# Mirrored rows in blocks of 32 instead of 16, with a VectorE shuffle in place of fp32 matmuls, in an attention and Fourier-mixing kernel

## The chip, the cores and the metric

The kernel runs on one core of a Trainium2 chip. A core has a tensor engine for matrix products (TensorE; PE in the profile, PEld for its weight loads), a vector engine (VectorE, DVE), a scalar engine for activations (ScalarE, ACT), a general engine (GpSimd, POOL) and a queue engine that only issues transfers (SyncE, SP). Each of them works through its own instructions in order and waits for the others through semaphores. Transfers between DRAM and the on-chip memory, and DMA transposes within it, are issued by SP, ScalarE and GpSimd and carried out by 16 DMA engines that all share. The metric is the device time of one execution in microseconds (us), as the median of several runs.

## What is computed

There are 8 batches, 8 heads, 576 rows and 64 columns a head. The first half is attention with a feature map; the second is a two-dimensional Fourier transform (its real part), a normalisation and a two-layer network.

```
def phi(x):
    proj = x @ w_phi                                   # 64 -> 128
    proj = proj - max(abs(proj), axis=-1)
    return concat([exp(proj), exp(-proj)], axis=-1)

q_p, k_p = phi(q), phi(k)
kv = k_p^T v;  z = sum(k_p, rows)
attn = (q_p kv) / (q_p z + 1e-06)
x = heads of attn side by side                         # 8 x 576 x 512
u = x + real(fft(fft(x, rows), columns))
un = (u - mean(u)) / sqrt(var(u) + 1e-06)
out = u + max(un @ w_ch1, 0) @ w_ch2                   # 512 -> 2048 -> 512
```

All inputs and the output are float32; the products run in bf16 with sums in float32.

## The kernel before

**Rows.** The Fourier transform along the 576 rows is folded: row n and row 576 - n are added and subtracted. So the kernel keeps q's rows, and everything made of them, in five chunks of up to 128 partitions. Chunks 0 and 1 hold rows 1 to 256, chunks 2 and 3 rows 320 to 575, chunk 4 row 0 and rows 257 to 319. A row and its mirror have to lie in one partition. q is loaded in its natural order, two rows a partition (`make_q`, L293), and the mirroring is spread over two places: within blocks of 16 partitions, or of the order of blocks, an access pattern with a negative step does it when q is the moving operand of a product (`queries`, L587, and `project`, L658). But the maxima of |q w_phi| come from products in which q is the stationary operand, so that they lie in the loaded order; for them `weigh_q` (L559) multiplies by two 128x128 permutation matrices TURN, in fp32, and then takes two exps, one for chunks 0 to 3 and one for chunk 4. TURN is made by `constants` (L182, the loop at L224) from counts `pc_i`, `blk` and `tn`; `pc_i` and `blk` are also in the chain to `pc`, the row numbers from which the angles of the sines and cosines come.

**Stages of a batch.** k, q and v of the next batch are loaded and cast to bf16 by GpSimd (`fetch_k`, `fetch_q`, `fetch_v`; `load`, L282). `arrive_k` and `arrive` (L1308, L1324) let SP transpose k and q. `features` (L429) makes the products with w_phi and their exps, the maxima (`qmax`, L537, `kmax`, L505) and v scaled by the maxima of k (`scale_v`, L456, on GpSimd). `keyvalue` (L878) and `combine` (L983) are the attention's products, with `tg`, `cb`, `rd` on VectorE and the last multiplication (L1002) on GpSimd. `folded` (L898) and `mixing` (L1018) do the transform, `normalise` and `scales` (L1119, L1177) the normalisation, with UN transposed by SP. `forward` (L1213) is the network: for each of 16 parts of the hidden layer four products (psf, L1224) and a ReLU, then the second layer (pso, L1241, L1267) and the result into X, which `store` (L1197) sends out from SP's queue. The store of chunks 0 and 1 goes in eight pieces of 16 partitions.

**The first batch** has functions of its own (`load_first`, `first_features`, `first_heads`): raw float32 loads through SP, transposes by TensorE, and the maxima of q brought into the exponent by products with `pick` (L697) instead of `weigh_q`. While it runs, `stir` (L1334) issues 15 groups of four idle matmuls.

**The order.** PLAN is a string in which each letter lets one stream make its next step (`STREAMS`, L1347, with the number of steps for each batch; `step`, L1358). Each engine gets its instructions in the order in which the steps issue them. The streams: F network, M attention products and mixing, D folding, N normalisation, U scales, P the maxima of q (its last step is `weigh_q`), T products and exps of the features, R the maxima of k, S scaling of v, K V Q the loads, A B the transposes of q and k, W the weights of the network (first W1b, then W2b), C constants, H sines, Y idle matmuls, G J the first batch's transposes, Z fills of padding (the fifth is HI). Places in PLAN are counted from 0 below.

Of the kernel before, what the change touches and what calls it, by code (L numbers as in the profile page):

```python
# [9 lines left out]
AT = mybir.ActivationFunctionType  # L10
# [13 lines left out]
    "CCZCYYZYGGCTZVTRZKGTGRZWGJTTSJYRSJTQTTPPYTYRPTJMRJTMSMMSPSTKPTPTZMYTMMQTMTPMCQTMMTMTBDMHKMHKHDDHYAHY"  # L24
    "DYMYMHYTMMVMRTQMTNMMYTNTQNNYSFNMFNFNRVRFSTTPTFMFRSYUNTFWMURFVFFFFUUMTPMFBSTFMNTUTPNUSMFVPPCTFMFTUPQM"
    "TFMFTFPATVMFFFMMFTFMFKMFFMQFMFRTKFMFFRFPFDFFFFTFFFFTDFFFDRTFFFMFFTTDMFRFFFFSFFMFFFTFMSMFRFTMTTNMTFMN"
    "FPTMMFSSMTPMFTPPMTFFFMFFQNMPTFBSFMFFQMFFPTFFMNNUAMFFMFMFVTRTFFMFFVRVFFKMFKFFFFTMFMFFFFQMFPFDFFTPFRFF"
    "FTFDPFFTFFDDFFRFFTMFFFTMFFMMBSFFMSFRFTMMTFTNNFMFMMMKFTFMTSTFFFFSMPPTMTFFFFFMFSFMFPTMQQVFFFPTKFFMNNNM"
    "FFMFFMFFUMFFMFMFFFAMTRTVFFRTVFFFFFQMFFFDFDFTFFFDRFTPDFFFTPFFRFFTMFFFFTMMMFSFFRSFTMFTFMTTFNFTFMFNSMMM"
    "FMBSFKTTMQNFFFNPFMTFFFMFTPPFMFSFMNFPQMUTFVFKFPAFFMMFMFFVMFFMTFMFFMFFFMRTFRVFFTFFFQMFFFFTDDFRFFFFTFDP"  # L30
    "FFDFTPFFFRFTMTFFFFFMMMFFRFSFSTMSTFFMTFTFFNMFFTNMMMMSTTFMFFQNFTFPMFFFMFVNFMTBPPFSFMFFTPFMKFFFMFFQPNMF"
    "FMAUKFFMFFFMTTFRFRFMFFFTSFFFFVTMFFFRMTQFFFMTFFFFDFDFFFRFDFTFFDMFTFMFFMFSMFMRFTFFTMFTFTFFTMNNFPSMMMMV"
    "TFFSMTPMSTQFFMTPMFTFBQMFPPPFFMFFMFNVFPFFANNUMFFMFMTFMFFMFFMFFRTFRMFFFFFFFVTTPFSFFRFVFFMTFDFFTFFFDFDR"
    "FFFFFTDMTMFFFFFMMFFSFRFTMFTTTMNFMTNMFFFFMSFMMPSTFMFFFNFPTMFFFFFFMTPPSFMFFMFPTFMFFPNFFTMFNMFFMFMFFUFM"
    "FMFFFFMMFFFFFFMFFFFDFFFDFDFFFDFMFFMFFMFFMMFFMNMFFNFFFFFFMFMFMFFFFFFFFFFFFFFFFFFFNFFFFFNFNFFFUFFFFFFF"
    "FFFFFFFFFFFFFFFFFFFFFFFFFFFFFFFFFFFFFF"
# [4 lines left out]
def kernel(  # L41
# [66 lines left out]
    TURN = const.tile([128, 2, 128], F32, name="TURN")  # L108
# [11 lines left out]
    pc_i = const.tile([128, 2], I32, name="pc_i")  # L120
    pc = const.tile([128, 5], F32, name="pc")
    pn = const.tile([128, 4], F32, name="pn")
    blk = const.tile([128, 3], F32, name="blk")
    tn = gs[:, 2048:2304].rearrange("p (t n) -> p t n", t=2)
# [23 lines left out]
    def count_first():  # L148
        count(pc_i[:, 0:1], [[1, 1]], 0, 1)
        count(pc[:, 0:2], [[1, 2]], 225, 2)  # L150
        count(pc[:, 2:3], [[1, 1]], 256, 1)
        nc.gpsimd.memset(pc[0:1, 2:3], 0.0)
        for j in range(2):
            count(
                rs[:, 128 * j:128 * j + 128].rearrange("p (a r) -> p a r", r=16),
                [[-32, 8], [2, 16]], 225 + j, 0,
            )
        count(rs[:, 256:NK], [[1, 64]], 256, 0)
        nc.gpsimd.memset(rs[:, 256:257], 0.0)
        count(tn[:, 0, :], [[1, 128]], 0, -1)  # L160
        nc.vector.tensor_single_scalar(
            out=ident[:], in_=tn[:, 0, :], scalar=0.0, op=ALU.is_equal
        )
        count(pc[:, 3:4], [[1, 1]], 128, -1)
        count(rc.rearrange("p (a r) -> p a r", a=2), [[1, 2], [2, 256]], 0, 0)

    def count_rest():
        count(pick_i[:], [[1, 32]], 0, -1)
        nc.vector.tensor_single_scalar(
            out=pick_i[:], in_=pick_i[:], scalar=31, op=ALU.bitwise_and  # L170
        )
        nc.vector.tensor_scalar(
            out=pick[:], in0=pick_i[:], scalar1=0.0, scalar2=-2.0, op0=ALU.is_equal, op1=ALU.mult
        )
        nc.vector.tensor_copy(out=ident_b[:], in_=ident[:])
        count(tn[:, 1, :], [[1, 128]], 0, 1)
# [5 lines left out]
    def constants(b):  # L182
        nc.vector.tensor_single_scalar(
            out=pc_i[:, 1:2], in_=pc_i[:, 0:1], scalar=4, op=ALU.arith_shift_right
        )
        nc.vector.tensor_copy(out=blk[:, 0:1], in_=pc_i[:, 1:2])
        nc.vector.scalar_tensor_tensor(
            out=pc[:, 0:2], in0=blk[:, 0:1].to_broadcast([128, 2]), scalar=-64.0,
            in1=pc[:, 0:2], op0=ALU.mult, op1=ALU.add,
        )  # L190
# [102 lines left out]
    def make_q(b):  # L293
# [4 lines left out]
            (QS[:], q[b, :, at:at + 256, :].rearrange("h (p j) d -> p h (j d)", j=2))  # L298
            for QS, at in ((QS01, 1), (QS23, 320))
# [129 lines left out]
    def features(b):  # L429
# [129 lines left out]
        def weigh_q(hs):  # L559
            n = hs.stop - hs.start  # L560
            pt = pk.tile([128, n, 4], F32, tag="pk", name="pt")
            for t in range(2):
                nc.tensor.matmul(
                    pt[:, :, 2 * t:2 * t + 2], lhsT=TURN[:, t, :],
                    rhs=mq[:, hs, 2 * t:2 * t + 2], start=True, stop=True,
                )
            nc.scalar.activation(
                out=E2[:, hs, 4:5], in_=mq[:, hs, 4:5], func=AT.Exp, scale=2.0
            )
            nc.scalar.activation(out=E2[:, hs, 0:4], in_=pt[:], func=AT.Exp, scale=2.0)  # L570
# [65 lines left out]
    def first_features():  # L636
# [21 lines left out]
        def project(ps, t, outer, last):  # L658
            for x, pr in enumerate((0, 3) if outer else (1, 2)):
                for jj in range(2):  # L660
                    rr = slice(64 * jj, 64 * jj + 64)
                    rq = (QT01, QT23)[t][rr, 2 * pr:2 * pr + 2, :]
                    rq = rq.rearrange("p h (a r) -> p h a r", r=16)
# [25 lines left out]
        def negative(t, outer):  # L689
            ps = pj.tile([128, 2, 4, 128], F32, tag="pj", name="psn")  # L690
            project(ps, t, outer, False)
            m = rows_of_m[outer][:].rearrange("p (a r) -> p a r", r=16)
# [504 lines left out]
    def store(b, U, c):  # L1197
        if c == 1:
            for a in range(8):
                queue = nc.scalar if b == B - 1 and a % 2 else nc.sync  # L1200
                queue.dma_start(
                    out=out[b, 225 - 32 * a:257 - 32 * a, :].rearrange("(r j) n -> r j n", j=2),
                    in_=U[16 * a:16 * a + 16, 0:2, 0:C],
                )
        elif c in (2, 3):
            rows_ = out[b, 320:576, :].rearrange("(a r j) n -> a r j n", r=16, j=2)
# [6 lines left out]
    def forward(b):  # L1213
# [68 lines left out]
        rows_ = out[b, 320:576, :].rearrange("(a r j) n -> a r j n", r=16, j=2)  # L1282
# [61 lines left out]
    def fold_later(b):  # L1344
# [7 lines left out]
        "C": (constants, 6), "H": (sines, 6), "Y": (stir, 15), "G": (turn_first_k, 5), "J": (turn_first_q, 5), "Z": (pads, 6),  # L1352
# [54 lines left out]
```

## Time and profile before

| | |
|---|---|
| median of 3 runs | 426.52 us (426.04 to 428.52) |
| span of the profiled execution, first to last instruction | 423.1 us |
| time around the span, by the median | 3.4 us |
| instructions | 10390 |
| TensorE's granted clock | 0.999 |
| DMA | 42.70 MB, mean 101 GB/s |

The profile has one execution of the program. No time of its own is listed for the profiled execution; what lies around its span is taken as the difference to the median. A row of grouped instructions reads: line, engine, operation, output<-inputs, shapes, xcount | busy us, mean ns of one | idle time of the engine just before them and what ended it. A row of the timeline starts with start and duration in us; a row of the chain of waits likewise, and it lists in order of time the work that the end of the run goes back to. A row of the busy time by stage gives the stretch, its length, for each engine the busy time and the number of instructions, then the granted clock, the mean busy share of the 16 DMA engines and GB/s. Matmuls are pipelined, so their busy times overlap.

### The profile page before, as it was taken

The page shows a single profiled execution, that of the slowest core. Times are in us where ns is not written, and L with a number is a line of the kernel's source. Part 1 is how long each engine was busy: PE and PEld are TensorE (multiplying, and loading weights), DVE is VectorE, ACT ScalarE, POOL GpSimd, SP SyncE. Part 2 cuts the span into 40 slices and gives each one's busy share as a digit, 9 for nine tenths or more (in the row PEclk, how much of TensorE's full clock was granted, in tenths as well). Part 3 has the DMA queues.
Part 4 walks back from the last instruction along what each step waited for, and adds up shares of the span by engine and source line. Part 5 has one row for each costly group of instructions (what it writes and reads, how often), then busy time and mean ns, then how long its engine had stood idle before and what let it go on. Part 6 is the DMA issues. An engine that isn't in the chain of part 4 may idle for free.

```text
span 423.1 us, 10390 instructions
## 1 busy us (share of the span) xinstructions
PE 397.4 (94%) x4093; PEld 256.1 (61%) x4122; DVE 331.1 (78%) x681; ACT 306.3 (72%) x626; POOL 207.8 (49%) x271
## 2 busy tenths in 40 slices
PE   8787798999899999999999999999999999999995
PEld 3454475744676558655675558665766567656563
DVE  4989788798979976998779885898989786968103
ACT  6978799748975899489847898588868887353460
POOL 7982688525646077706673282834755331500000
PEclk9999999999999999999999999999999999999999
DMA  8999959984569468853899069954895081103313
GB/s 218 206 165 163 148 88 174 145 83 76 89 102 180 72 101 106 123 84 49 112 153 138 2 91 136 131 71 66 117 138 77 14 102 32 27 0 72 72 26 87
DMA packets 108761, 42.70 MB, mean 101 GB/s; under 512 B 82857, under 2 KB 103721, under 8 KB 108713
## 3 DMA queue, kind: packets, MB, share of 16 engines
q0 software_dynamic: 45936, 16.60, 37.1%
q1 hardware_dynamic: 62215, 24.85, 34.8%
q8 instruction: 32, 0.52, 0.5%
q10 hardware_dynamic: 562, 0.59, 0.5%
q14 instruction: 16, 0.13, 0.1%
HBM read 36.77 MB, written 9.44 MB: 109 GB/s over the span
## 4 chain that ended last, share of the span: by engine, by line
PE 61%; DVE 20%; ACT 8%; POOL 5%; DMA 2%; issue 2%; DVEq 0%; ACTq 0%; POOLq 0%
PE psf L1224 21%; PE pso L1241 19%; DVE R L903 3%; PE kv L887 3%; DVE cb L999 3%; DVE tg L994 2%; PE pso L1267 2%; PE psD L1045 2%; DMA UT<-UN 2%; PE pu L1104 2%; PE psq L547 1%; DVE MK L511 1%; PE psk L491 1%; PE psh L597 1%; DVE X L1094 1%
## 5 line engine op out<-in xcount | busy, mean ns | idle before, releaser
L1224 PE MATMUL psf<-UT,W1b 128*128 128x320 bf16 (+1 forms) x1024 | 142.5, 286 | 2.4 <-DMA UT<-UN 1.5
L1241 PE MATMUL pso<-W2b,HT 128*128 128x512 bf16 x467 | 117.1, 379 | 1.7 <-issue 0.5
L1224 PEld LDWEIGHTS <-W1b 128*128 128x128 bf16 x1024 | 94.0, 98 | 29.7 <-issue 4.3
L1229 ACT ACTIVATE HT<-psf 128x320 bf16<-128x320 f32 x128 | 53.5, 442 | 27.0 <-PE psf L1224 21.6
L1241 PEld LDWEIGHTS <-HT 128*128 128x128 bf16 x496 | 44.8, 98 | 44.6 <-issue 2.6
L1002 POOL TENSOR_TENSOR X<-cb,rd 128x320 f32<-128x320 f32 x56 | 41.5, 746 | 38.6 <-DVE rd L1001 37.3
L466 POOL TENSOR_TENSOR VCn<-VS,VCn 128x512 bf16<-128x512 bf16 x28 | 29.7, 1061 | 38.1 <-ACT VCn L461 35.3
L1231 ACT ACTIVATE HT<-psf 128x512 bf16<-128x512 f32 x64 | 37.9, 605 | 12.6 <-PE psf L1224 12.0
L555 DVE TENSOR_REDUCE MQ<-psq 128x8 f32<-128x1024 f32 (+1 forms) x32 | 34.3, 1084 | 13.4 <-PE psq L547 13.2
L1247 DVE SCALAR_TENSOR_TENSOR X<-pso,rs,X 128x512 f32<-128x512 f32 x31 | 22.8, 735 | 21.6 <-PE pso L1241 21.6
L497 ACT ACTIVATE KPn<-psk 128x1024 bf16<-128x1024 f32 x28 | 28.6, 1021 | 14.0 <-DVE MK L511 13.9
L497 ACT ACTIVATE KPp<-psk 128x1024 bf16<-128x1024 f32 x28 | 28.7, 1025 | 11.1 <-PE psk L491 11.1
L451 POOL TENSOR_TENSOR V4N<-VS,V4N 64x256 bf16<-64x256 bf16 x14 | 8.7, 623 | 53.9 <-ACT V4N L447 53.4
L511 DVE TENSOR_REDUCE MK<-psk 128x8 f32<-128x1024 f32 x28 | 33.9, 1212 | 1.0 <-ACT KPp L497 0.7
L1094 DVE TENSOR_TENSOR X<-pu,X 128x512 f32<-128x512 f32 (+3 forms) x49 | 23.3, 526 | 11.2 <-PE pu L1104 8.9
L466 POOL TENSOR_TENSOR VCp<-VS,VCp 128x512 bf16<-128x512 bf16 x28 | 29.7, 1059 | 0.0
L606 ACT ACTIVATE QPHP<-psh 128x1024 bf16<-128x1024 f32 x28 | 28.9, 1031 | 0.8 <-PE psh L597 0.6
L606 ACT ACTIVATE QPHN<-psh 128x1024 bf16<-128x1024 f32 x28 | 29.0, 1035 | 0.0
L1150 ACT ACTIVATE UN<-X,MV 128x512 bf16<-128x512 f32 (+1 forms) x35 | 24.5, 723 | 5.4 <-DVE MV L1175 3.1
L1174 DVE BATCH_NORM_STATS2 st<-X 128x6 f32<-128x512 f32 (+1 forms) x40 | 27.1, 677 | 0.3
L1190 POOL TENSOR_TENSOR rs<-VE,mhalf 128x5 f32<-128x5 f32 (+1 forms) x9 | 10.3, 1145 | 29.0 <-DVE VE L1189 29.0
L987 PEld LDWEIGHTS <-QPHP 128*128 128x128 bf16 x280 | 21.2, 99 | 4.6 <-DVE cb L999 1.0
(465 smaller groups left out, 825.0 us busy)
## 6 DMA issues: line engine op xcount, KB each, us to landing
out_dram<-X SPq DMA_DIRECT2D x15, 256.0 KB
out_dram<-X SPq DMA_DIRECT2D x60, 64.0 KB
QS<-in_q_dram POOLq DMA_DIRECT2D x14, 256.0 KB, 6.2
KS<-in_k_dram POOLq DMA_DIRECT2D x7, 512.0 KB, 7.4
VS<-in_v_dram POOLq DMA_DIRECT2D x14, 256.0 KB, 5.1
W1b<-in_moe_w_ch_dram POOLq DMA_DIRECT2D x1, 2048.0 KB, 13.1
W2b<-in_moe_w_ch_dram POOLq DMA_DIRECT2D x1, 2048.0 KB, 14.8
W2b<-in_k_dram SPq DMA_DIRECT2D x2, 512.0 KB
```

The source lines that it names most:

```text
L466: nc.gpsimd.tensor_tensor(out=VC[:, hs, :, 0:D], in0=values[b][0][:, hs, :].rearrange("p h (j d) -> p h j d", d=D), in1=VC[:, hs, :, D:D + ...
L497: nc.scalar.activation(out=KP[:, hs, :, :].rearrange("p e (jp jj) f -> p jj (e jp) f", jj=2), in_=psk[:], func=AT.Exp, scale=sgn,)
L511: nc.vector.tensor_reduce(out=MK[:, 2 * pr:2 * pr + 2, :].rearrange("p e (jp jj) -> p jj (e jp)", jj=2), in_=tiles[pr][:], axis=AX.X, op=A ...
L555: nc.vector.tensor_reduce(out=o, in_=i[:], axis=AX.X, op=ALU.max, apply_absolute_value=True)
L606: nc.scalar.activation(out=o, in_=psh[:], func=AT.Exp, scale=sgn)
L1002: nc.gpsimd.tensor_tensor(out=X[:, :, D * h:D * h + D], in0=cb[:, :, 0:D], in1=rd[:].to_broadcast([128, 5, D]), op=ALU.mult,)
L1094: nc.vector.tensor_tensor(out=to, in0=more, in1=to, op=ALU.add)
L1174: nc.vector.bn_stats(out=st[0:M, :], in_=X[0:M, c, 0:C])
L1224: nc.tensor.matmul(ps, lhsT=W1b[:, cc, 128 * hh:128 * hh + 128], rhs=UT[:, cc, lo:hi], start=(cc == 0), stop=(cc == NCC - 1),)
L1229: nc.scalar.activation(out=HT[:, hh, lo:hi], in_=ps, func=AT.Relu, scale=-1.0)
L1231: nc.scalar.activation(out=HT[:, hh - 1:hh + 1, lo:hi], in_=psw[:].rearrange("p (a n) -> p a n", a=2), func=AT.Relu, scale=-1.0,)
L1241: nc.tensor.matmul(po[:], lhsT=HT[:, hh, at:at + 128], rhs=W2b[:, hh, :], start=(hh == 0), stop=(hh == NHH - 1),)
```

## The change

The blocks are 32 partitions wide, the width within which a VectorE shuffle can move data between partitions. The order of blocks in chunks 0 and 1 is turned by the load: `make_q` loads them in four pieces, the last rows first. Only the mirror within a block, for chunks 2 and 3, is left for the maxima, and `weigh_q` does it in place with one shuffle and takes one exp over all five chunks. TURN, `pc_i`, `blk` and one half of `tn` go. The store of chunks 0 and 1 goes in four pieces. The first batch keeps its loads and takes 32 for 16 in its patterns. PLAN is a new order of the same steps (one C step fewer).

```diff
 PLAN = (
-    "CCZCYYZYGGCTZVTRZKGTGRZWGJTTSJYRSJTQTTPPYTYRPTJMRJTMSMMSPSTKPTPTZMYTMMQTMTPMCQTMMTMTBDMHKMHKHDDHYAHY"
-    "DYMYMHYTMMVMRTQMTNMMYTNTQNNYSFNMFNFNRVRFSTTPTFMFRSYUNTFWMURFVFFFFUUMTPMFBSTFMNTUTPNUSMFVPPCTFMFTUPQM"
...
+    "YYKCCZVYCYZGGTZTTRGZGCRGTTSJRYTJSPTYPTRJYTSPTVJMRTSMMJPPTTPTMMMTTSKQMMTPQCZMMMTTMTDMMQWYDHYHBYAYDDHY"
+    "HMHMTKMMTRHMTMMTQNVMTYYNQNSKNNFRZFTFFRNMNYPSFUTFMTFFUMRTWFSFMNFFTRNQUPFFSFSMTPMTNPFBUVPMPTTMFFTMTVPF"
...
     def count_first():
-        count(pc_i[:, 0:1], [[1, 1]], 0, 1)
-        count(pc[:, 0:2], [[1, 2]], 225, 2)
+        for a in range(4):
+            count(pc[32 * a:32 * a + 32, 0:2], [[1, 2]], 193 - 64 * a, 2)
...
-        count(tn[:, 1, :], [[1, 128]], 0, 1)
...
     def constants(b):
-        nc.vector.tensor_single_scalar(
-            out=pc_i[:, 1:2], in_=pc_i[:, 0:1], scalar=4, op=ALU.arith_shift_right
-        )
-        nc.vector.tensor_copy(out=blk[:, 0:1], in_=pc_i[:, 1:2])
-        nc.vector.scalar_tensor_tensor(
-            out=pc[:, 0:2], in0=blk[:, 0:1].to_broadcast([128, 2]), scalar=-64.0,
-            in1=pc[:, 0:2], op0=ALU.mult, op1=ALU.add,
-        )
...
-        for t, n in enumerate((112.0, 15.0)):
-            nc.vector.tensor_scalar(
-                out=blk[:, 1 + t:2 + t], in0=pc_i[:, 1:2], scalar1=64.0 * t - 32.0,
-                scalar2=n, op0=ALU.mult, op1=ALU.add,
-            )
-            nc.vector.tensor_scalar(
-                out=TURN[:, t, :], in0=tn[:, t, :], scalar1=blk[:, 1 + t:2 + t], scalar2=None,
-                op0=ALU.is_equal,
-            )
-        yield
...
         pieces = [
-            (QS[:], q[b, :, at:at + 256, :].rearrange("h (p j) d -> p h (j d)", j=2))
-            for QS, at in ((QS01, 1), (QS23, 320))
+            (QS[:], q[b, :, at:at + 64 * n, :].rearrange("h (p j) d -> p h (j d)", j=2))
+            for QS, at, n in [
+                (QS01[32 * a:32 * a + 32], 193 - 64 * a, 1) for a in range(4)
+            ] + [(QS23, 320, 4)]
         ]
...
         def weigh_q(hs):
-            n = hs.stop - hs.start
-            pt = pk.tile([128, n, 4], F32, tag="pk", name="pt")
-            for t in range(2):
-                nc.tensor.matmul(
-                    pt[:, :, 2 * t:2 * t + 2], lhsT=TURN[:, t, :],
-                    rhs=mq[:, hs, 2 * t:2 * t + 2], start=True, stop=True,
-                )
-            nc.scalar.activation(
-                out=E2[:, hs, 4:5], in_=mq[:, hs, 4:5], func=AT.Exp, scale=2.0
-            )
-            nc.scalar.activation(out=E2[:, hs, 0:4], in_=pt[:], func=AT.Exp, scale=2.0)
+            nc.vector.stream_shuffle(
+                out=mq[:, hs, 2:4], in_=mq[:, hs, 2:4], mask=list(range(31, -1, -1))
+            )
+            nc.scalar.activation(out=E2[:, hs, :], in_=mq[:, hs, :], func=AT.Exp, scale=2.0)
...
                 if t:
-                    rq = rq.rearrange("p h (a r) -> p (h a) r", r=16)[:, :, ::-1]
-                else:
-                    rq = rq.rearrange("p h (a r) -> p h a r", r=16)[:, :, ::-1, :]
+                    rq = rq.rearrange("p h (a r) -> p (h a) r", r=32)[:, :, ::-1]
...
         if c == 1:
-            for a in range(8):
+            for a in range(4):
                 queue = nc.scalar if b == B - 1 and a % 2 else nc.sync
                 queue.dma_start(
-                    out=out[b, 225 - 32 * a:257 - 32 * a, :].rearrange("(r j) n -> r j n", j=2),
-                    in_=U[16 * a:16 * a + 16, 0:2, 0:C],
+                    out=out[b, 193 - 64 * a:257 - 64 * a, :].rearrange("(r j) n -> r j n", j=2),
+                    in_=U[32 * a:32 * a + 32, 0:2, 0:C],
                 )
...
     def fetch_q(b):
         staged[b], pieces = make_q(b)
-        for which in ((0,), (1,), (2, 3)):
+        for which in ((0, 1, 2, 3), (4,), (5, 6)):
             load(pieces, which)
             yield
...
-        "C": (constants, 6), "H": (sines, 6), "Y": (stir, 15), "G": (turn_first_k, 5), "J": (turn_first_q, 5), "Z": (pads, 6),
+        "C": (constants, 5), "H": (sines, 6), "Y": (stir, 15), "G": (turn_first_k, 5), "J": (turn_first_q, 5), "Z": (pads, 6),
```

In the order of the steps, the first W stands at place 86 instead of 23, the first Q at 67 instead of 35, the fifth Z at 74 instead of 22, and the first K at 2 instead of 17; the rest of PLAN keeps nearly the same sequence of steps in each batch, moved by a few places.

More of the change, by code (lines that the diff above doesn't have):

```diff
@@ L29 @@
[L29 to L33, printed above, removed]
@@ L119 @@
     rc, rs = gc[:, 0:C], ga[:, 3 * NK:4 * NK]
-    pc_i = const.tile([128, 2], I32, name="pc_i")
     pc = const.tile([128, 5], F32, name="pc")
     pn = const.tile([128, 4], F32, name="pn")
-    blk = const.tile([128, 3], F32, name="blk")
-    tn = gs[:, 2048:2304].rearrange("p (t n) -> p t n", t=2)
+    tn = gs[:, 2048:2176]
     ident = const.tile([128, 128], F32, name="ident")
@@ L154, in count_first @@
             count(
-                rs[:, 128 * j:128 * j + 128].rearrange("p (a r) -> p a r", r=16),
-                [[-32, 8], [2, 16]], 225 + j, 0,
+                rs[:, 128 * j:128 * j + 128].rearrange("p (a r) -> p a r", r=32),
+                [[-64, 4], [2, 32]], 193 + j, 0,
             )
@@ L159, in count_first @@
         nc.gpsimd.memset(rs[:, 256:257], 0.0)
-        count(tn[:, 0, :], [[1, 128]], 0, -1)
-        nc.vector.tensor_single_scalar(
-            out=ident[:], in_=tn[:, 0, :], scalar=0.0, op=ALU.is_equal
-        )
+        count(tn, [[1, 128]], 0, -1)
+        nc.vector.tensor_single_scalar(out=ident[:], in_=tn, scalar=0.0, op=ALU.is_equal)
         count(pc[:, 3:4], [[1, 1]], 128, -1)
```

27 lines of the change are left out of this document (15 added, 12 removed).

## The prediction

> **What bounds the kernel now.** I read the page first, then busy time by stage, then the chain of waits.
>
> ```profile
> span 423.1 us, 10390 instructions
> ...
> PE 397.4 (94%) x4093; PEld 256.1 (61%) x4122; DVE 331.1 (78%) x681; ACT 306.3 (72%) x626; POOL 207.8 (49%) x271
> ```
> ```profile
> core 0: us, PE busy (x) PEld busy (x) DVE busy (x) ACT busy (x) POOL busy (x), PEclk, DMA share, GB/s
> 0.00:75.00 75.00, 60.75 (x730) 38.79 (x730) 59.73 (x138) 63.48 (x124) 55.76 (x86) 1.00 1.06 167
> 75.00:386.00 311.00, 304.48 (x3144) 196.16 (x3169) 262.71 (x527) 229.35 (x477) 150.84 (x184) 1.00 0.70 89
> 386.00:423.10 37.10, 32.16 (x230) 21.11 (x226) 8.67 (x16) 13.50 (x27) 1.17 (x1) 0.99 0.30 66
> ```
> There are two regimes. From 75 to 386 us TensorE is the bound: busy 304.48 of 311, so 6.52 us are seen to be lost there, and whatever leaves its queue in this stretch shortens the run. In the first 75 us no engine is full: ScalarE has 63.48, TensorE 60.75 (of which much is the program's own idle matmuls, "idle" on L1338), VectorE 59.73, GpSimd 55.76, and the DMA engines are saturated (share 1.06). There the chain of waits decides. The last 37 us are TensorE again and then the last store; their instructions hardly change.
>
> **Part 1: the mirror of the maxima.** `weigh_q` issues four fp32 matmuls for each batch of 1 to 7 (two products in two passes) and two exps; it becomes one shuffle and one exp.
>
> ```profile
> 74.58 0.35 PE pt L563 x4
> ```
> ```profile
> core 0: us, PE busy (x) PEld busy (x), PEclk, DMA share, GB/s
> 0.00:75.00 75.00, 0.52 (x4) 0.55 (x4) 1.00 1.06 167
> 75.00:386.00 311.00, 3.10 (x24) 3.15 (x24) 1.00 0.70 89
> ```
> In the chain four of them take 0.35 us of TensorE. Six of the seven groups lie in the dense stretch (24 of 28 matmuls) and one at its edge: 7 x 0.35 = 2.45, say **-2.5**. Their busy time of 3.10 + 0.52 = 3.6 is the upper bound (each is drawn with its pipeline's length); the lower is 0, if the places were waits anyway. In exchange VectorE gets a shuffle of 128x16 fp32, which this trace doesn't have. The nearest short row is the 128x20 subtraction below, 0.18 us alone; its stretched twin (0.98) and the 128x20 cast (2.32) are what such an instruction costs beside a GpSimd tensor operation. So 0.18 to 2.32; I take 0.18, as in batches 1 to 7 the maxima come long after the GpSimd work of their batch, or 1.3 in all.
>
> ```profile
> 22.08 2.32 DVE L730 CAST m<-MQ 128x20 bf16<-128x20 f32 x1
> ...
> 24.43 0.18 DVE L731 TENSOR_TENSOR ml<-MQ,m 128x20 f32<-128x20 f32 x1
> ...
> 28.93 0.98 DVE L731 TENSOR_TENSOR ml<-MQ,m 128x20 f32<-128x20 f32 x1
> ```
> ```profile
> L567 ACT ACTIVATE E<-MQ 128x8 f32<-128x8 f32 x7 | 1.6, 226 | 0.0
> ...
> L570 ACT ACTIVATE E<-pt 128x32 f32<-128x32 f32 x7 | 1.5, 209 | 0.3
> ```
> VectorE is busy 262.71 of 311 in the dense stretch, so its 1.3 is covered by its idle time; without that cover it costs 1.3. ScalarE loses one of two exps, 7 x 0.21 = 1.5, also off the path. The shuffle follows the reduction on the same engine, and behind it in VectorE's queue stand the products `tg`, which need the exp and so the shuffle anyway: no wait is added on another engine. The PSUM buffer "pk" is used once less a batch. Net of these **+0.2** (-1.5 to +1.3, and +16 if all seven were stretched to 2.32).
>
> The Trainium skill, "Vector Engine (DVE) Microarchitecture Reference", section 3.8, says that a shuffle reads mask bytes which an instruction of its own has to load before, so that each mirror would be two VectorE instructions. No run here shows it yet; at 0.18 each that would be 2.5 us on VectorE instead of 1.3, still less than its idle time.
>
> **Part 2: the start.** `pc_i` and `blk` go: three small VectorE instructions that stand in the chain before GpSimd can begin with the angles.
>
> ```profile
> 3.56 0.07 DVE pc_i L183
> ...
> 3.65 0.16 DVE blk L186
> ...
> 3.84 0.17 DVE pc L187
> ```
> They are worth 0.07 + 0.16 + 0.17 = **-0.4**. GpSimd's counting ahead of it changes by one small instruction (three leave: pc_i, pc, one of tn; four of 32x2 come): 0.
>
> **Part 3: GpSimd in the first batch.** GpSimd scales v there (L852, L869), and its queue carries loads and fills in front of that.
>
> ```profile
> 14.78 1.01 POOL L274 MEMSET HI<- 128x512 bf16 x2
> 15.71 0.79 POOL L93 DMA_DIRECT2D W1b<-in_moe_w_ch_dram  x1
> ...
> 21.33 0.93 POOL L284 DMA_DIRECT2D QS<-in_q_dram  x1
> ...
> 25.76 1.06 POOL L869 TENSOR_TENSOR VCn<-HT,VCn 128x512 bf16<-128x512 f32 x1 [1.40 <-ACT VCn L862]
> ...
> 29.82 0.92 POOL L284 DMA_DIRECT2D KS<-in_k_dram  x1
> ...
> 31.03 2.36 POOL L284 DMA_DIRECT2D QS<-in_q_dram  x3
> ...
> 53.59 1.04 PE L1224 MATMUL psf<-UT,W1b 128*128 128x256 bf16 x8
> ```
> The new order puts the fill of HI, the load of W1b and the first load of q behind the scaling (steps Z, W, Q: places 22, 23 and 35 become 74, 86 and 67): 1.01 + 0.79 + 0.93 = 2.7 less in front. One load of v comes before its end (+0.8), and the small load of k goes to the very front, into the time in which GpSimd waits for pc. So the scaling ends 1.9 earlier, and up to 3.3 if the wait of 1.40 for ScalarE closes too: the second pair of exps (step S, place 55) now stands at 50, before the evictions that it was queued behind. What takes over is VectorE:
>
> ```profile
> 20.00:35.00 15.00, 12.95 (x228) 9.33 (x225) 13.03 (x26) 11.77 (x27) 12.70 (x16) 1.00 1.03 165
> 35.00:41.00 6.00, 4.44 (x56) 2.44 (x53) 5.86 (x14) 4.53 (x7) 0.00 (x0) 1.00 1.58 169
> 41.00:54.00 13.00, 9.47 (x76) 5.27 (x76) 9.92 (x30) 10.14 (x21) 6.69 (x12) 1.00 1.39 148
> ```
> It has 13.03 busy of 15, so 2 us to give, and a little more where its casts are no longer stretched by GpSimd. I take **-1.6** (0 to -3.3).
>
> **Part 4: the idle matmuls.** Three of their groups stand in the chain of waits:
>
> ```profile
> 28.37 0.86 PE idle L1338 x4
> ...
> 42.10 0.88 PE idle L1338 x4
> ...
> 43.02 1.04 PE idle L1338 x4
> ...
> 44.10 0.42 PE ps L477 x8
> ```
> The old order has two Y steps between the sum along rows (M at place 102) and the first product of batch 1 (T at 107); the new one has none there (M 101, T 104) and issues them earlier, where TensorE waits anyway. That brings the product at 44.10 forward by 1.9. But VectorE folds from 35 to 46 without a break (5.86 of 6), and the next evictions on ScalarE need that: half of it, **-0.9** (0 to -1.9). The one at 28.37 falls in with part 3.
>
> **Part 5: loads, stores, constants.** q goes in four pieces of 32 partitions: three more GpSimd issues a batch.
>
> ```profile
> L284 POOL DMA_DIRECT2D QS<-in_q_dram x28: 560/910/957, 21.3 to 303.1; - x28
> ```
> ```profile
> QS<-in_q_dram POOLq DMA_DIRECT2D x14, 256.0 KB, 6.2
> ...
> W1b<-in_moe_w_ch_dram POOLq DMA_DIRECT2D x1, 2048.0 KB, 13.1
> ...
> QS<-in_q_dram POOLq DMA_DIRECT2D x7, 1.0 KB, 5.4
> ```
> A piece has a quarter of the rows: between the 0.56 of the one-row load and the 0.96 of the full one, so 3 x 0.56 to 3 x 0.96 = 1.7 to 2.9 a batch, 12 to 20 in all. GpSimd is busy 150.84 of 311 in the dense stretch, and in the new order these steps stand mostly outside the run of products that TensorE's later work needs, which hides it: **+0.3** (0 to +12). The store of c = 1 is four issues of 128 KB, not eight of 64:
>
> ```profile
> 242.04 5.13 SPq L1201 DMA_DIRECT2D out_dram<-X  x8
> ```
> ```profile
> 248.62 3.74 DMA UT<-UN
> ```
> Eight take 5.13 on SP's queue, and the transposes UT stand behind them; four save 2.6 a batch if one costs as before, 0 if twice that. UT is on the chain in two batches: **-0.5** (0 to -2). The TURN tables (four VectorE instructions near 70.5) are under ScalarE, 0. W1b is issued later: the scaling ends near 28, and behind it stand k, four pieces of q, q23, HI and two more: 28 + 0.92 + 2.8 + 0.93 + 1.01 + 1.43 = 35.1. With 13.1 to land that is 48.2, before its first use at 53.59. For a share of DMA of 1.39 I add **+0.4**.
>
> **Sum:** -2.5 + 0.2 - 0.4 - 1.6 - 0.9 + 0.3 - 0.5 + 0.4 = -5.0. The profiled span is 423.1, the median of the runs 426.52 (426.04 to 428.52), so 3.4 lies around the span and stays: 418.1 + 3.4 = **421.5**. The rest of the new order moves steps by a few places; each batch begins after nearly the same number of F steps, so I take 0 for it.
>
> **Rivals.** (a) *Only the matmuls count.* VectorE's density in 20 to 46 us swallows parts 3 and 4, as its rows allow: -2.5 - 0.4 = 423.6. Against it: 2 us of idle there, and a cast stretched to 2.32. (b) *The order also closes waits in the dense stretch.* Half of the 6.52: 421.5 - 3.3 = 418.2. For it: small waits are spread over all batches; against: the old order has no worse cadence. (c) *W1b comes too late, slower than before.* If it needs twice 13.1 and starts only when the q pieces in front have landed (6.2), it lands at 35.1 + 6.2 + 26.2 = 67.5; TensorE, in order, stands at the first L1224 for 13.9: 435.4. It decides from a landing 5.4 + 5.0 = 10.4 us later than mine, at 58.6. For it: a DMA share of 1.39 to 1.58 in 35 to 54. Against: the same bytes are only moved, and those before 28 us become fewer by as much. (d) *The four pieces are not hidden.* GpSimd is late by 1.7 in each of seven batches: 421.5 + 11.9 = 433.4 at most, 427.5 at half.
>
> The Trainium skill, "DMA: Bandwidth & Descriptors", section "Anatomy of one DMA", speaks for (d): a GpSimd-issued DMA costs some 2.0 us whatever its size, so by it four pieces one after another would be an estimated 6 us later than one. Here a 1 KB load takes 5.4 and a 256 KB load 6.2 with others in flight: most is fixed, as that rule has it, but it overlaps.
>
> **How the numbers follow.** Chances: the forecast 0.45 (419.5 to 423.5; two thirds of it under 422.25), (b) 0.20, (a) 0.17, (c) 0.08, (d) 0.10, of which 0.06 within and 0.04 above. One per cent, 4.3 us, is about what a measurement of this kernel can tell from no change. Faster 0.30 + 0.20 = 0.50, same 0.15 + 0.17 + 0.06 = 0.38, slower 0.12. The range 416.0 to 427.5 holds the forecast, (a), (b) and the milder half of (d).
>
> **What would show it.** Right: no `pt<-MQ,TURN` rows, seven shuffles under 0.4 us, the product now at 44.10 near 41 to 42, the first L1224 near 50, and 75:386 shorter by about 2.5 with TensorE as dense. Part 3 is wrong if the last L869 ends after 28.5. The forecast is wrong if TensorE's first wait for W1b is over 4 us, if GpSimd's waits move to its own DMA issues, or if the dense stretch loses more than 8 us.

## The result and the profile after

The changed kernel takes 441.72 us (439.43 to 445.68, 4 runs); the kernel before took 426.28 us (425.17 to 428.52, 4 runs) beside it. The ratio is 1.037 (1.031 to 1.044): 15.4 us slower, where 5.0 us faster was forecast. The profiled execution took 439.43 us, with a span of 437.6. Ratios here and below compare undisturbed executions only, so where the executions of a kernel scatter, the ratio can lie below that of the two medians.

The page of the changed kernel begins:

```profile
span 437.6 us, 10330 instructions
...
PE 401.5 (92%) x4064; PEld 256.0 (58%) x4094; DVE 328.4 (75%) x688; ACT 306.1 (70%) x619; POOL 217.0 (50%) x293
```

TensorE has fewer instructions and yet more busy time than before (397.4). The busy time by stage, in the prediction's stretches, says why: the granted clock (the column behind POOL) is no longer 1.00. From 75 to 386 us TensorE is now idle for 19.4 us, where it was 6.52; the prediction had named a loss of more than 8 there as a sign that it is wrong.

```profile
0.00:75.00 75.00, 63.88 (x702) 39.15 (x702) 55.73 (x131) 60.93 (x118) 56.26 (x91) 0.93 1.01 155
75.00:386.00 311.00, 291.64 (x3052) 187.76 (x3078) 254.29 (x521) 226.31 (x462) 159.62 (x201) 0.98 0.73 91
```

Where the time goes is seen best by marking progress: the start of the n-th of the 1024 products psf with W1b (L1224 before, L1193 after; lines lie 22 to 31 lower in the changed kernel), in us from the span's start.

| n | before | after | difference |
|---|---|---|---|
| 0 | 53.6 | 52.4 | -1.2 |
| 64 | 69.9 | 72.7 | +2.8 |
| 96 | 78.3 | 90.9 | +12.6 |
| 256 | 158.2 | 175.8 | +17.5 |
| 512 | 252.4 | 267.3 | +14.9 |
| 1023 | 409.1 | 423.0 | +13.9 |

The start is ahead, the stretch behind n = 256 gives back 3.6, and all the loss falls between 52 and 176 us: 4.0 near 60 us, 9.8 near 80, and 4.9 more from n = 96 to 256, where TensorE waits 5.7 us for the transposes UT and in the kernel before not at all. Why UT comes late there was not followed; the experiments below go after the two steps ahead of it. In the chain of waits of the changed kernel two pieces of the same kind stand there, both the transposes of q; in the chain of before neither is there.

```profile
37.37 13.86 DMA QT<-QS
...
74.72 11.72 DMA QT<-QS
```

SP's timeline shows them (start, duration, line, operation). The duration is the time for which issuing a transpose holds SP's queue; no row tells when its data have arrived. In the kernel before:

```profile
39.52 1.25 SPq L420 DMA_TRANSPOSE QT<-QS  x1
...
57.52 3.50 SPq L410 DMA_TRANSPOSE KT<-KS  x2
70.97 1.24 SPq L420 DMA_TRANSPOSE QT<-QS  x1
73.97 2.37 SPq L421 DMA_TRANSPOSE QT<-QS  x1
```

And in the changed kernel:

```profile
37.37 9.16 SPq L398 DMA_TRANSPOSE QT<-QS  x1
46.69 3.45 SPq L399 DMA_TRANSPOSE QT<-QS  x1
...
64.44 10.04 SPq L388 DMA_TRANSPOSE KT<-KS  x2
74.72 4.11 SPq L398 DMA_TRANSPOSE QT<-QS  x1
78.94 3.05 SPq L399 DMA_TRANSPOSE QT<-QS  x1
```

The same transpose holds the queue for 9.16 us instead of 1.25, another pair for 10.04 instead of 3.50. Each slow one starts 2.5 to 3.7 us behind the issue of a 2 MB load from GpSimd's queue, and ends 12.5 to 12.8 us behind it:

```profile
33.71 0.81 POOL L93 DMA_DIRECT2D W1b<-in_moe_w_ch_dram  x1
...
61.96 1.20 POOL L95 DMA_DIRECT2D W2b<-in_moe_w_ch_dram  x1
```

Who waits is in the list of waits up to 100 us (us in total, times, longest). Behind the first slow one it is GpSimd's next load of q, with the scaling of v and fills of padding (DT) queued behind it, and through a fill TensorE; behind the second it is TensorE itself, at the maxima of batch 2.

```profile
POOL QS L260 <- DMA QT<-QS: 9.3, 1, 9.3
...
PE psq L525 <- DMA QT<-QS: 8.4, 1, 8.4
...
PE pu L1073 <- POOL DT L253: 2.5, 1, 2.5
```

That made a first theory: the new order puts transposes under 2 MB loads, W1b's over batch 1 and W2b's over batch 2. The rivals: the new parts themselves cost it, or the new order is bad in another way.

### The profile page after: what moved, and what is told of

Its sections match the earlier page's. It is cut to its first block, busy times and chain, and to the rows that moved or that the text cites. A ratio compares the mean times of both kernels' runs of the same rounds, so it can differ in the third digit from the quotient of the medians.

```text
span 437.6 us, 10330 instructions
## 1 busy us (share of the span) xinstructions
PE 401.5 (92%) x4064; PEld 256.0 (58%) x4094; DVE 328.4 (75%) x688; ACT 306.1 (70%) x619; POOL 217.0 (50%) x293
## 4 chain that ended last, share of the span: by engine, by line
PE 61%; DVE 18%; DMA 10%; ACT 5%; issue 2%; POOL 2%; SPq 1%; DVEq 0%; POOLq 0%; ACTq 0%
PE psf L1193 24%; PE pso L1210 15%; DMA QT<-QS 6%; DMA UT<-UN 4%; DVE cb L968 4%; PE kv L856 3%; DVE tg L963 3%; PE psD L1014 2%; PE pso L1236 2%; DVE R L872 2%; PE pu L1073 2%; PE psk L469 2%; PE idle L1307 1%; PE psq L525 1%; PE psh L566 1%
## 5 line engine op out<-in xcount | busy, mean ns | idle before, releaser
L1193 PE MATMUL psf<-UT,W1b 128*128 128x320 bf16 (+1 forms) x1024 | 143.0, 289 | 7.2 <-DMA UT<-UN 6.2
L1193 PEld LDWEIGHTS <-W1b 128*128 128x128 bf16 x1024 | 95.7, 99 | 36.3 <-issue 5.4
L1200 ACT ACTIVATE HT<-psf 128x512 bf16<-128x512 f32 x64 | 37.8, 601 | 15.4 <-PE psf L1193 15.2
L260 POOL DMA_DIRECT2D QS<-in_q_dram x49 | 33.0, 680 | 9.3 <-DMA QT<-QS 9.3
L1159 POOL TENSOR_TENSOR rs<-VE,mhalf 128x5 f32<-128x5 f32 (+1 forms) x9 | 10.2, 1138 | 34.8 <-DVE VE L1158 34.7
```

The lines of the kernel that those rows point to most:

```text
L260: nc.gpsimd.dma_start(out=pieces[i][0], in_=pieces[i][1])
L1193: nc.tensor.matmul(ps, lhsT=W1b[:, cc, 128 * hh:128 * hh + 128], rhs=UT[:, cc, lo:hi], start=(cc == 0), stop=(cc == NCC - 1),)
L1200: nc.scalar.activation(out=HT[:, hh - 1:hh + 1, lo:hi], in_=psw[:].rearrange("p (a n) -> p a n", a=2), func=AT.Relu, scale=-1.0,)
```

## The experiments

Edits of PLAN are shown by the letters around the place that changes. Differences in us are to the kernel before as timed beside each run (median 425.2 to 426.4); those to the changed kernel carry that spread of the kernel before, up to 1.1 us.

**The new parts in the old order** (`e1_parts_old_order`) and **the new order with the old parts** (`e3_order_alone`): the changed kernel with the PLAN of before, less one C; and the kernel before with the new PLAN and a C added at place 190.

> All parts of the change (blocks of 32, shuffle, q in four pieces, stores in four), with the order of steps of the kernel before (its last constants step left out, as that step is gone). Theory A, the new order is what costs: 423.5 us (420 to 426), the transposes QT of batch 1 at about 1.3 us each on SP's queue, as before. Theory B, the parts cost (four pieces of q hold up GpSimd and the transposes): 435 us or more, with GpSimd waiting for QT or its issues on the chain.

> The kernel before, with the new order alone (the sixth constants step, which it still has, put at place 190). Theory A: 443 us (439 to 447), with the same slow transposes. Theory B: 425 to 428 us.

Measured: 431.63 us (427.97 to 434.67), ratio 1.012 (1.007 to 1.017), for the parts; 458.79 us (456.52 to 463.83), ratio 1.075 (1.072 to 1.079), for the order. So the parts lose some 5 us by themselves, and the larger loss comes with the order. The order with the old parts is worse than both together: it loses again from n = 256 on (19 us there, 33 at the end), with four waits of psf for the transposes UT, 12.3 us in all from 100 to 420 us, where the kernel before has 1.5. Why UT comes late there was not followed.

**W1b's place alone**, in both directions. `e2_w1b_early` puts it back in the changed kernel, `e4_w1b_late` moves it in the kernel before.

```diff
 e2, changed kernel, places 20 and 84
-GCRGTTS   MMQWYDH
+GCRWGTTS  MMQYDH
 e4, kernel before, places 20 and 83
-GRZWGJTT  TBDMHKM
+GRZGJTT   TBDMWHKM
```

> The changed kernel, with one letter of the order moved: the load of W1b back to place 23 from place 86. Theory A1, the 2 MB of W1b lying over the transposes of q for batch 1 is the cause: QT back to 1.2 to 1.5 us each, no wait of GpSimd of 9 us for QT, 424 us (421 to 428). Theory A2, the order as a whole (k of batch 2 late, W2b over the transposes of batch 2): QT of batch 1 is fast but 432 to 438 us remain. Theory B: 439 to 444 us.

> The kernel before, with one letter moved: the load of W1b from place 23 to place 86. Theory A1: the transposes of q for batch 1 take 3 us or more on SP's queue and the time rises to 434 us (430 to 441). Theory A2: the old order has slack enough behind it, 425 to 429 us. Theory B: 426 us.

Measured: 434.42 us (432.62 to 435.10), ratio 1.019 (1.016 to 1.022), 7.3 less than the changed kernel; and 432.67 us (432.40 to 433.19), ratio 1.016 (1.014 to 1.018), 7.0 more than before. SP's timeline of `e4_w1b_late`, whose W1b is issued at 32.54 us:

```profile
35.19 10.52 SPq L410 DMA_TRANSPOSE KT<-KS  x2
45.88 3.32 SPq L420 DMA_TRANSPOSE QT<-QS  x1
```

GpSimd's next load of k waits for these transposes, and TensorE for a fill queued behind that load (its waits from 40 to 110 us):

```profile
PE psD L1045 <- POOL SS L254: 8.2, 1, 8.2
```

The one letter costs 7 us in either kernel, and the first psf does not wait for W1b in any of them. In `e2_w1b_early` the transposes of batch 1 are quick again, those of batch 2 are not:

```profile
37.89 1.23 SPq L398 DMA_TRANSPOSE QT<-QS  x1
...
59.08 10.17 SPq L388 DMA_TRANSPOSE KT<-KS  x2
69.47 4.11 SPq L398 DMA_TRANSPOSE QT<-QS  x1
```

**How much of a load is met** (`e6_w1b_halves`): the kernel before with W1b in two loads of 1 MB.

```diff
-        nc.gpsimd.dma_start(out=W1b[:], in_=moe_w_ch1.rearrange("(j p) h -> p j h", p=128))
+        w1 = moe_w_ch1.rearrange("(j p) h -> p j h", p=128)
+        nc.gpsimd.dma_start(out=W1b[:, 0:NCC // 2, :], in_=w1[:, 0:NCC // 2, :])
+        yield
+        nc.gpsimd.dma_start(out=W1b[:, NCC // 2:NCC, :], in_=w1[:, NCC // 2:NCC, :])
         yield
...
-        "W": (load_ffn_weights, 2),
+        "W": (load_ffn_weights, 3),
 PLAN, place 83
-TBDMHKM
+TBDMWHKM
```

> The kernel before, with W1b loaded in two halves of 1 MB: the first at place 23 as before, the second at place 87, where all of it was put in the run with W1b late. Theory (a transpose that meets a load waits until the load's bytes have landed): the transposes of k for batch 1 take 4 to 7 us, between 3.45 and 10.5, and the time is 1 to 4 us over before: 427 to 430. Rival (any load issued just ahead costs the same, whatever its size): 10 us and 432 to 433. Rival 2 (half the bytes are hidden): 425 to 427.

Measured: 429.75 us (428.44 to 429.91), ratio 1.009 (1.007 to 1.011). Its transposes:

```profile
36.29 6.55 SPq L413 DMA_TRANSPOSE KT<-KS  x2
43.01 2.03 SPq L423 DMA_TRANSPOSE QT<-QS  x1
```

With none, half and all of W1b issued just ahead, the pair holds SP's queue for 3.45, 6.55 and 10.52 us, and the run costs 0, 3.4 and 7.0: both go with the bytes issued ahead.

**Out from under W2b** (`e5_w1b_k2_early`, then `e9_w1b_k2_q2_early`): W1b early, and batch 2's big load of k earlier, so that its transposes come ahead of W2b; then its small loads of q ahead of W2b as well.

```diff
 e5, beside e2's edit: places 103 and 122
-MTKMMTRHM   YNQNSKNNFR
+MTKKMMTRHM  YNQNSNNFR
 e9, beside these: places 122 and 160
-YNQNSNNFR   MNFFTRNQUPFF
+YNQQNSNNFR  MNFFTRNUPFF
```

> The changed kernel with two steps moved back: the load of W1b to place 23, and the big load of k for batch 2 from place 127 to 106, so that its transposes stand ahead of the load of W2b. Theory (the whole loss is two meetings of the DMA transposes with a 2 MB load): the transposes of batch 2 that took 10.2 us under W2b take about 3.5, TensorE's wait of 9 us for QT near 70 to 80 us goes, the first product with W1b stays near 50.5 us, and what the dense stretch gave back in the run with W1b early (3.6) is kept: 418 to 423 us. Rival 1 (the earlier load of k holds GpSimd, and VS and the scaling of v come late in its place): 425 to 430. Rival 2 (the new order is slow by itself in batch 2): 432 to 435, as with W1b early alone.

> The changed kernel with three steps moved back: W1b to place 23, the big load of k for batch 2 to 106, and the two small loads of q for batch 2 (63 KB and 1 KB) from place 167 to 125, so that nothing which batch 2's first products need is queued behind W2b. Theory: those loads land before W2b is issued, TensorE's wait of 4.8 us for QT near 74 to 79 us goes, and with it the half clock from 78 to 85; the start stays 1 to 3 us ahead of before and the dense stretch gives back 0.5 to 3: 421 to 426 us, and less where no half clock falls near 44 us. Rival (the DMA engines have the same bytes to move from 42 to 80 us, so the wait moves to another transfer, VS or QT01): 428 to 432.

Measured: 432.60 us (430.26 to 438.25), ratio 1.014 (1.010 to 1.018); and 436.74 us (430.10 to 438.57, 4 runs), too scattered for a ratio. In `e5_w1b_k2_early` the transposes hold SP's queue only briefly:

```profile
58.19 2.62 SPq L388 DMA_TRANSPOSE KT<-KS  x2
70.35 1.24 SPq L398 DMA_TRANSPOSE QT<-QS  x1
71.70 3.97 SPq L399 DMA_TRANSPOSE QT<-QS  x1
```

But TensorE's timeline of the same run still has the wait:

```profile
78.97 0.61 PE L525 MATMUL psq<-wphi,QT 64*128 64x128 bf16 x8 [4.85 <-DMA QT<-QS]
```

And `e9_w1b_k2_q2_early`, with no load of k or q for batch 2 behind W2b, has 5.02 us there. So moving these loads ahead is not enough. That does not clear W2b: a short issue is not a short transfer. What the DMA queues moved in `e5_w1b_k2_early` between the issue of q's transposes, at 70.35 us, and the beginning of TensorE's wait, at 74.12 (queue: packets, MB, share of 16 engines):

```profile
DMA packets 1246, 0.75 MB, mean 198 GB/s; under 512 B 564, under 2 KB 1246, under 8 KB 1246
...
q0 software_dynamic: 1246, 0.75, 133.5%
```

All of it went over GpSimd's queue (q0); SP's (q1), which carries the transposes, has no row, and its first packet comes at 74.4. In `e9_w1b_k2_q2_early` it stands still from 76.6 to 80.1 in the same way, and in the kernel before from 71.0 to 74.8, 12.9 us behind W2b's issue, where nobody waits for it. So q's transposes still stood behind GpSimd's loads in both runs, for 4.0 and 3.6 us of waits of 4.85 and 5.02, and the first theory is not refuted by them.

The other half of that wait is a reader too close behind the issue: in the new order the first maxima of batch 2 (a P) stand at place 210, five places and 2 F steps behind the A at 205 that issues q's transposes; before it was 239 behind 207, with 14 F steps between. In batches 3 to 7 the two orders have 16 to 47 F steps there.

**The step of the first maxima alone**, again in both directions: `e12_p2_late` moves only it in the changed kernel, `e15_p2_early_before` in the kernel before; `e13_w1b_early_p2_late` joins it with W1b early.

```diff
 e12 (and e13, beside e2's edit), changed kernel, places 205 and 235
-AMTFFPUFTMM  VFQFFRF
+AMTFFUFTMM   VFQFFPRF
 e15, kernel before, places 206 and 235
-PATVMFFFMM   FRFPFDF
+PATVMFFPFMM  FRFFDF
```

> The changed kernel with one step moved: the first maxima of batch 2 from place 210 to 239, so that 14 forward steps instead of 2 stand between the issue of q's transposes and their first reader. Theory (the transposes of batch 2 have no cover in the new order): the wait of 8 to 9 us for QT near 76 to 86 us and the half clock after it go, W1b's meeting stays: 430 to 434. Rival (only W2b's load over the transposes matters, and the step's place does not): 439 to 442.

> The kernel before with one step moved: the first maxima of batch 2 from place 239 to 213, 2 forward steps behind the issue of q's transposes as in the new order. Theory: TensorE waits 4 to 7 us for QT near 75 to 82 us, and the time is 430 to 434. Rival (transposes of 1.2 to 2.4 us, as they are in the kernel before, are soon enough): 425.5 to 428.

> The changed kernel with that step moved and W1b's load back at place 23. Theory (these two causes are nearly all of the loss): 421 to 426. Rival (the transposes of k that last 10 us under W2b still hold TensorE): 428 to 432, with a wait for KT or QT of more than 3 us in batch 2.

Measured: `e12_p2_late` 430.16 us (429.39 to 431.30), ratio 1.010 (1.006 to 1.013), 11.6 less than the changed kernel; `e15_p2_early_before` 431.78 us (430.90 to 433.20), ratio 1.015 (1.010 to 1.019), 6.5 more than before; `e13_w1b_early_p2_late` 425.97 us (423.81 to 430.83, 10 runs), ratio 1.000 (0.998 to 1.003). TensorE's waits from 60 to 110 us in `e15_p2_early_before`:

```profile
PE psq L547 <- DMA QT<-QS: 4.0, 1, 4.0
```

Its transposes hold SP's queue for 1.23 and 2.63 us, as in the kernel before; SP's queue moves nothing from 70.9 to 74.7, and TensorE waits until 80.2.

And in `e13_w1b_early_p2_late`, first SP's timeline and then TensorE's longest wait in the same stretch:

```profile
59.32 10.12 SPq L388 DMA_TRANSPOSE KT<-KS  x2
69.67 4.11 SPq L398 DMA_TRANSPOSE QT<-QS  x1
73.89 4.23 SPq L399 DMA_TRANSPOSE QT<-QS  x1
```

```profile
PE psk L469 <- ACT KPn L475: 0.8, 1, 0.8
```

The pair issued behind W2b holds SP's queue as long as ever (10.12), and TensorE does not wait for it: the 16 F steps that now stand between cover it. So the place of the P decides whether W2b's hold on the transposes is paid in batch 2, with a wait of 8 to 9 us where k's transposes come behind W2b too and of 4 to 5 where they come ahead of it. What the early P would cost with W2b's load elsewhere was not tried.

With two letters, W and P, moved back, the changed kernel is level with the kernel before. That is a balance, not the end of all losses: in the old order the parts alone cost 5.0 us, so the rest of the new order gains about as much.

**The shuffle alone** (`e7_shuffle_alone`) and **the four pieces of q alone** (`e8_q_pieces_alone`), each in the kernel before:

```diff
 e7, weigh_q
-            (the two products with TURN and the two exps)
+            nc.vector.stream_shuffle(
+                out=mq[:, hs, 2:4], in_=mq[:, hs, 2:4],
+                mask=list(range(15, -1, -1)) + list(range(31, 15, -1)),
+            )
+            nc.scalar.activation(out=E2[:, hs, :], in_=mq[:, hs, :], func=AT.Exp, scale=2.0)
 e8, make_q
+            (QS01[32 * a:32 * a + 32],
+             q[b, :, 1 + 64 * a:65 + 64 * a, :].rearrange("h (p j) d -> p h (j d)", j=2))
+            for a in range(4)
```

> The kernel before with the shuffle and one exp in place of the four fp32 matmuls and two exps, within blocks of 16; order, loads and stores as before. It leaves out the swap of the blocks among themselves in the first two columns of maxima, and still makes the TURN tables. Forecast of the prediction (part 1): 2.3 us less, 423 to 424. Rival (TensorE is held by the evictions behind it, so that the 2.5 us come back as waits for ScalarE): 425 to 426.5, with some 2 us more of TensorE's waits for the evictions in the dense stretch. Rival 2 (the one exp stands behind the shuffle and holds ScalarE's queue): over 426.5.

> The kernel before with q's first half in four loads of 32 partitions (64 KB) in place of one of 256 KB; all else as before. Theory (GpSimd hides them): 425 to 426.5, with 1.4 to 2 us more of GpSimd's time for each batch. Rival (they make the scaling of v late in batch 1, and what hangs on it): 427 to 430, with the first product with W1b 1.5 to 4 us later than 53.6.

Measured: the shuffle, in a kernel that leaves out the swap of the blocks, 423.06 us (422.59 to 426.23, 10 runs), ratio 0.994 (0.992 to 0.996), 2.6 us by the ratio; the pieces 430.73 us (430.20 to 431.46), ratio 1.012 (1.010 to 1.013), 4.9 us by the ratio. The two add up to 2.3 of the 5.0 us that all parts cost in the old order; the other 2.7 (the stores and the start's constants were not tried alone) stay open. In the profiled execution of the pieces TensorE loses 2.3 us up to the first psf and 3.1 behind it. Of the 2.3 a part is a half clock that begins at 16.6 us, ahead of the first changed instruction; the 3.1 fall in small steps in each batch. By the stage's row GpSimd has 160.58 us busy from 75 to 386 us, 150.84 before:

```profile
75.00:386.00 311.00, 303.62 (x3162) 194.92 (x3162) 259.59 (x517) 230.28 (x479) 160.58 (x202) 1.00 0.71 90
```

**The idle matmuls** (`e11_idle_early`, `e10_and_idle_late`, `e16_two_more_idle`) and **all moves together** (`e14_five_moves`).

```diff
 e11, kernel before, place 92
-DDHYAHYDYMYMHYTMM
+DDHYYYAHYDYMMHTMM
 e10, beside e9's edits: place 94
-AYDDHYHMHMTKKMMTRHM
+ADDHHMHMYTKKMMYTRHM
 e14: e9's edits and e12's
 e16, beside e14's edits: place 100, and 17 steps of Y instead of 15
-HMHMTKKMMTRHM
+HMHMYTKKMMYTRHM
```

> The kernel before with part 4 alone: the two steps of idle matmuls between the sum along rows and the first product of batch 1 (places 103 and 106) are put ahead of place 96. Prediction (part 4): 0.9 us less (0 to 1.9), 424.5 to 426.4. Rival (they keep the clock up): a half clock after 43 us in some or all executions, 427 to 428.5 in those, and a scatter of 2 us and more.

> The same as the run with the three steps moved back, with two steps of idle matmuls put later too, from ahead of the mixing's sum (places 95 and 99) to between its products (104 and 108), where TensorE stood idle from 39.6 to 43.4 us. Theory (that idle time is what lets the clock fall to half near 44 us in some executions): no half clock between 40 and 55 us, a smaller scatter, and a median 1 to 2 us under that run. Rival (the idle matmuls only delay the products behind them, as the prediction's part 4 has it): 0.9 to 1.9 us over it.

> The changed kernel with five steps moved back: W1b's load to 23, batch 2's big load of k to 106 and its small loads of q to 125, its first maxima to 239. Theory: no wait of TensorE for QT or KT above 1 us in batch 2, 419 to 424, and under the kernel before. Rival (the start's half clocks and the four pieces of q keep what the dense stretch gains): 425 to 428.

> The run with five moves, with two steps of idle matmuls added (17 instead of 15), ahead of places 104 and 108, none taken away elsewhere. Theory (TensorE under half busy for 3.4 us lets the clock fall to half, and the new order opened such a place at 39.5 to 43.4 us): fewer executions with a half clock, a median of 422 to 426 us, below the run with five moves (428.05), and a smaller scatter than its 15 us. Rival (the half clocks have another cause, or fall elsewhere): the median within 1.5 us of 428, with the same scatter, or 1 to 2 us higher by the added matmuls.

Measured: `e11_idle_early` 426.44 us (424.18 to 428.32, 10 runs), ratio 1.000 (0.998 to 1.002); `e10_and_idle_late` 436.21 us (432.37 to 440.75), ratio 1.019 (1.013 to 1.025), as scattered as `e9_w1b_k2_q2_early`; `e14_five_moves` 428.05 us (422.12 to 437.05, 12 runs), ratio 0.998 (0.995 to 1.001); `e16_two_more_idle` 432.57 us (423.44 to 439.82, 12 runs), ratio 0.999 (0.996 to 1.002). Part 4 of the change, by itself, is worth nothing that the interval (0.9 us less to 1.0 more) tells from zero. With five moves the profiled execution has no half clock until its last 3 us, a span of 420.3 and 422.12 us in all, under every run of the kernel before beside it (424.64 at least); but most other executions show a lower clock and up to 437. Two more groups of idle matmuls did not help: in that run's profile the half clock came at another place, from 161.6 us, behind a wait of 6.0 us for UT. So the theory that the idle matmuls' place causes the scatter fell, and what causes it stays open. No version here that computes the whole function beats the kernel before by its median.

The marks of progress for the runs that carry the argument, as differences to the kernel before in us:

| n | after | W1b early (e2) | P late (e12) | both (e13) | five moves (e14) |
|---|---|---|---|---|---|
| 0 | -1.2 | -3.1 | -3.1 | -3.1 | -2.9 |
| 64 | +2.8 | -3.2 | +4.0 | -3.2 | -3.2 |
| 96 | +12.6 | +7.5 | +3.2 | -4.0 | -3.9 |
| 256 | +17.5 | +10.9 | +9.7 | +3.3 | +0.6 |
| 1023 | +13.9 | +7.3 | +5.9 | +0.9 | -3.2 |

Neither letter takes away the loss from n = 96 to 256: it is 7.3 us with both moved and 4.5 with five moves, TensorE waits there for UT for 3.6 and 4.2, and the stretch behind gives back 2.4 and 3.8.

## Why the prediction was wrong

**The step that failed most** is a sentence behind the sum: "The rest of the new order moves steps by a few places; each batch begins after nearly the same number of F steps, so I take 0 for it." It counted F steps to the beginning of a batch, not from the issue of a transfer to its first reader. For batch 2 that distance went from 14 F steps to 2, behind a transfer that moved no byte for some 4 us (`e5_w1b_k2_early`, `e15_p2_early_before`). Measured: 11.6 us in the changed kernel, 6.5 in the kernel before. How much of it W2b's load adds stays open.

**The second step** is W1b in part 5: "W1b is issued later", +0.4. Part 5 asked only whether W1b lands before its first use, and rightly found that it does. The price is paid by others: the transposes issued just behind it, and through them GpSimd's queue and TensorE. No term and no rival had them. Measured: 7.0 and 7.3 us.

**The third** is the four pieces of q, +0.3 (0 to 12). Measured: 4.9 by the ratio. Rival (d) had the size (6 at half, 11.9 at most), with a chance of 0.10. The page's row for these loads, beside the 23.2 us for 28 before:

```profile
L260 POOL DMA_DIRECT2D QS<-in_q_dram x49 | 33.0, 680 | 9.3 <-DMA QT<-QS 9.3
```

The 680 ns are the mean of all 49 loads; their median is 0.59 us, and 28 of them are pieces, so a piece lies inside the bounds (0.56 to 0.96), near the lower one. That idle time on GpSimd hides the pieces was wrong in the old order. Of what the Trainium skill says there, "DMA: Bandwidth & Descriptors", section "Anatomy of one DMA" (2.0 us for each), the runs show only that the number of loads counts: a 64 KB piece lands 5.3 us after its issue.

**Part 1 was right**: -2.3 forecast, -2.6 measured. VectorE's groups in the changed kernel (busy us, mean ns):

```profile
L538 DVE STREAM_SHUFFLE MQ<-MQ 128x16 f32<-128x16 f32 x7 | 1.4, 195 | 0.0
L538 DVE LOAD_MASK_SELECT MQ<-MQ x7 | 0.1, 14 | 0.3
```

The shuffle takes the 0.18 that was taken for it, and never a stretched time (193 to 198 ns in all seven). The Trainium skill's second instruction ("Vector Engine (DVE) Microarchitecture Reference", section 3.8) is there, at 14 ns.

**Parts 2 and 3.** GpSimd's timeline has the first of the angles and the last scaling of v:

```profile
4.50 1.56 POOL L183 TENSOR_SCALAR gs<-ga,pn 128x320 f32<-128x320 f32 x3 [0.17 <-DVE pn L178]
...
26.16 1.05 POOL L838 TENSOR_TENSOR VCp<-HT,VCp 128x512 bf16<-128x512 f32 x1
```

The angles start at 4.50, not 0.4 earlier than before but 0.1 later (4.39): GpSimd's counts of the row numbers, for which the prediction took 0, now last 0.88 us (0.13 and 0.23 before), and VectorE waits for the counts. The scaling ends at 27.21, 2.7 before the old one (29.88), inside its 0 to 3.3.

**Part 4** moved the product from 44.10 to 39.51, more than the 41 to 42 expected. TensorE's timeline shows what became of it:

```profile
34.01 5.35 PE L1307 MATMUL idle<-ones_b 128*128 128x512 bf16 x20
...
39.51 0.41 PE L455 MATMUL ps<-wphi,KT 64*64 64x128 bf16 x8
41.13 1.01 PE L1014 MATMUL psD<-SS,CEO 128*128 128x289 bf16 x6 [1.22 <-DVE CEO L1003]
42.08 0.40 PE L469 MATMUL psk<-wphi,KT 64*128 64x128 bf16 x8
43.27 1.38 PE L1014 MATMUL psD<-CS,CEO 128*128 128x289 bf16 x6 [0.79 <-DVE CEO L1003]
```

The next products wait for VectorE's folding, as the prediction feared for one half of it. Parts 2 to 4 together were to bring 2.9 by the first psf; with W1b early, 3.1 came. That the sum fits is partly luck: part 2 brought nothing, and part 3 more than was taken for it.

**The sum redone** with the measured terms: -2.6 (part 1), -3.1 (parts 2 to 4), +4.9 (pieces), +7.3 (W1b), +11.6 (first maxima of batch 2) is +18.1, against +15.4 measured. Some of it overlaps: with W1b early, the P step gains 8.5 and not 11.6. The stores were not tried alone; four issues take 2.6 us of SP's queue in `e14_five_moves`, as forecast, but UT is on the changed kernel's chain in four batches, 17.2 us, and on that of before in two, 7.6.

## What to carry to other kernels

When an order of steps is rewritten, measure for each transfer the work between its issue and its first reader, batch by batch, and compare: one step moved from 32 places behind its transposes to 5 cost up to 11.6 us here. Ask of a big load not only whether it lands in time, but which small transfers are issued while it is in flight, on other queues too. Test a suspected cause both ways, taken out of the new kernel and put into the old one: that is what showed the price of each letter. And do not take a short issue for a short transfer: q's transposes of batch 2 held SP's queue for 1.24 us in the kernel before and moved their first byte 3.9 us after that issue began, so look at the bytes of the queue before you clear a load that is in flight.

## What the hardware showed beyond what was expected

The issue of DMA transposes on SP's queue is held up by a load on GpSimd's queue in step with its bytes: 3.45, 6.55 and 10.52 us for one pair, with 0, 1 and 2 MB issued 3 us ahead. A transpose issued later behind such a load can look free and still be held: in the kernel before, one issued 9.1 us behind W2b takes 1.24 us of SP's queue, but that queue's next packet comes 3.9 us after the issue, 12.9 us behind W2b's.

A wait of TensorE is paid for a second time by its clock. The busy time by stage of `e2_w1b_early`, cut where its granted clock changes:

```profile
72.00:75.40 3.40, 0.11 (x1) 0.00 (x0) 0.35 (x2) 1.94 (x5) 0.72 (x1) 1.00 1.38 167
75.40:85.60 10.20, 4.05 (x43) 2.71 (x44) 2.27 (x4) 1.52 (x3) 1.20 (x1) 0.50 1.07 99
85.60:89.00 3.40, 3.40 (x42) 2.58 (x40) 2.74 (x9) 1.95 (x5) 1.63 (x3) 1.00 0.00 0
```

After 3.4 us in which TensorE is busy for 0.11, the clock is at half for 10.2 us, and the products that follow the wait run at half speed. The Trainium skill, "TensorE: Matmul & The Clock Gate", Part 1, describes this: a free-running window of 3413 ns, and half the clock after an idle one. The trace agrees with the length: 10.2 us is three such windows. Which executions fall into it differs from run to run: with five moves, 422.12 us at a mean granted clock of 0.999, 425.1 at 0.992, 430.0 at 0.983.
